# Four bias stores and eight bias reads issued by GpSimd in place of SyncE, in an attention and feed-forward kernel on one core

## The chip, the cores and the metric

One core of one Trainium2 chip runs the whole kernel. The metric is device time in microseconds (us), the median of a few executions; beside it stands one profiled execution, whose trace is what is read here. The engines are named as in the trace: PE (TensorE), ACT (ScalarE), DVE (VectorE), POOL (GpSimd) and SP (SyncE, which only issues transfers here).

## The reference

Attention with a bias that depends on the two positions, then a feed-forward layer over the 2304 tokens:

```python
B, H, S, D = 4, 8, 576, 64
scores = q @ k^T / sqrt(D)
x      = log1p(|i - j|) / log1p(max(i, 1))          # i query, j key
bias   = relu(x * w1 + b1) @ w2                     # hidden 32, one value per head
attn   = softmax(scores + bias)
x      = (attn @ v) as (B*S, H*D)                   # 2304 x 512
h      = x @ w_in;  out = (h * sigmoid(h)) @ w_out  # d_ff 2048
```

## The kernel before

All instructions are laid out by a planner (`Plan`, line 203) before the program is built: every step is an operation with a due time, its engines, and the buffers it reads and writes; `order` (line 286) simulates them with estimated durations and writes them out in the order that results. Each engine then works through its own list in that order, and waits at an instruction until what it needs is there. A table (`SHIFT`, line 40) moves the due times of single groups.

The bias is made on the chip once. It has 36 tiles of 16 query rows each, `bias_tile(st, t0)` (line 487). Four `bias_f` steps (line 503 on ACT or line 505 on DVE) compute the hidden layer from a table of logarithms, SBUF to SBUF; matmuls (line 511) bring in w2; two evictions (`bias_ev`, line 518 on ACT or line 520 on DVE) scale the result out of PSUM into a tile `bsb` of 128 partitions by 591 values; and a store (`bias_st`, line 522) writes that tile to a scratch tensor in DRAM, `bias_d[c]`, with c = st // 8. In DRAM the rows are skewed, so that a later read with a shifted row pitch gives the bias of each query row by key. Chunks c = 0 to 3 have 128 query rows (8 tiles each); chunk c = 4 has the last 64 rows (tiles 32 to 35). Chunk 4 is done first: `PHASES` (line 26) begins with it, then come 0, 1, 2, 3 for batches 0 and 1, and later the two other batches.

In a phase, `visit` goes over four pairs of heads (hp) and the batches. `bias_of(hp, c, t0)` (line 640) gives the bias tile of a head pair, read from DRAM. For c = 4 the two heads of a pair lie in the two halves of the partitions, so there are two reads per pair (`ld_bias2`, line 654, 64 partitions by 576 values each) and, ahead of them, two memsets on POOL (lines 650 and 651) that fill the margins of the tile. For c < 4 there is one read per pair (line 657). A read must wait for the stores of all tiles of its chunk: it depends on `bias_b[c]`.

In `chunk` (line 746) the step "max" (line 795, on DVE) adds the scores in PSUM to the bias tile and takes the row maximum; "exp" (line 802, ACT), transposes (line 811, PE), evictions (lines 446 and 448) and the product with v (line 683, PE) follow. The feed-forward part (lines 867, 890, 974, 1058) is PE work beside and behind the attention.

Before the change all transfers are issued by SP, in one list. Each of its transfers signals one of eight semaphores in turn (DMAHW0 to DMAHW7 in the rows of the program), and an issue that is to use one of them again waits until the transfer eight places earlier has landed.

Of the kernel before, what the change touches and what calls it, by code (L numbers as in the profile page):

```python
# [387 lines left out]
def attention_moe_kernel(ctx: ExitStack, tc: tile.TileContext, q, k, k0, v, small, w_in, w_out, lut, ident_d, out):  # L388
    nc = tc.nc
    V, A, G, T, SP = nc.vector, nc.scalar, nc.gpsimd, nc.tensor, nc.sync  # L390
# [14 lines left out]
    def bias_at(c, at, dims, h=0, n=H):  # L405
        t = bias_d[c].rearrange("h i p -> (h i p)")
        size = bias_d[c].shape[1] * (BW + 15)
        return bass.AP(tensor=t.tensor, offset=t.offset + h * size + at, ap=[x or [size, n] for x in dims])

    bias_b = [Buf(None) for _ in range(5)]  # L410
# [12 lines left out]
    def buf(tag, shape, dtype=F32):  # L423
        return Buf(tag, shape, dtype)

    def bank(tag, n):
        return Buf(tag, banks=n)

    def tl(b):
        if b.banks:  # L430
            return psum[:, b.at, :] if b.banks == 1 else psum[:, b.at:b.at + b.banks, :].rearrange("p a n -> p (a n)")
        if b.t is None:
            n = 1
            for x in b.shape[1:]:
                n *= x
            flat = pools[b.tag].tile([128, sizes[b.tag]], b.dtype, tag=b.tag, name=b.tag)
            b.t = flat[:, 0:n]
            if len(b.shape) == 3:
                b.t = b.t.rearrange("p (a n) -> p a n", a=b.shape[1])
            if len(b.shape) == 4:  # L440
                b.t = b.t.rearrange("p (a b n) -> p a b n", a=b.shape[1], b=b.shape[2])
        return b.t
# [10 lines left out]
    def op(kind, where, prio, reads=(), writes=(), shy=6.0):  # L453
        def add(fn):
            plan.op(kind, where, prio, fn, reads, writes, shy=shy)
            return fn
        return add

    def load(kind, prio, writes, fn, bytes, reads=(), plain=False):
        plan.op(kind, ("SP", 0.45 if plain else 0.55), prio, fn, reads, writes, bytes)  # L460
# [26 lines left out]
    def bias_tile(st, t0):  # L487


        plan.group()  # L490
        lo, hi = 16 * st + 15, S - 16 * st
        n = max(lo + 1, hi)
        bps = bank("B", 1 if n <= 512 else 2)
        Fs = [buf("G", [128, 2, n]) for _ in range(2)]
        bsb = buf("G", [128, BW])
        fat = lambda i: tl(Fs[i // 2])[:, i % 2, :]
        for ig in range(4):
            @op("bias_f", {"ACT": 0.2 + n * 0.00083, "DVE": 0.13 + n * 0.00053},
                t0 + 0.3 * ig, reads=[lut_b, (cb, 0)], writes=[(Fs[ig // 2], ig)])
            def _(e, g=4 * st + ig, ig=ig):  # L500
                src = tl(lut_b)[:, 0:n]
                if e == "ACT":
                    A.activation(out=fat(ig), in_=src, func=AF.Relu, bias=beta(g))
                else:
                    ENG[e].tensor_scalar(out=fat(ig), in0=src, scalar1=beta(g), scalar2=0.0, op0=ALU.add, op1=ALU.max)

        @op("bias_mm", ("PE", n * 0.00167 + 0.1), t0 + 1.8, reads=[(Fs[i // 2], i) for i in range(4)] + [(cb, 0)], writes=[bps])
        def _(e):
            for x in range(0, n, 512):
                for ig in range(4):  # L510
                    T.matmul(out=tl(bps)[32 * ig:32 * ig + 32, x:min(n, x + 512)], lhsT=w2bd(), rhs=fat(ig)[:, x:min(n, x + 512)],
                             start=True, stop=True)

        @op("bias_ev", {"ACT": 0.3 + BW * 0.00083, "DVE": 0.24 + BW * 0.00103}, t0 + 2.5, reads=[bps, cb], writes=[bsb])
        def _(e):
            for x, d, w in ((tl(bps)[:, lo:0:-1], 0, lo), (tl(bps)[:, 0:hi], lo, hi)):
                if e == "ACT":
                    A.activation(out=tl(bsb)[:, d:d + w], in_=x, func=AF.Copy, scale=scale(st))
                else:
                    V.tensor_scalar_mul(out=tl(bsb)[:, d:d + w], in0=x, scalar1=scale(st))  # L520

        load("bias_st", t0 + 3.2, [(bias_b[st // 8], st)], lambda e: SP.dma_start(
            out=bias_at(st // 8, 16 * (st % 8) * (BW + 15), [[BW + 16, 16], None, [1, BW]]), in_=tl(bsb)), 302592, reads=[bsb])


# [61 lines left out]
    def keys(b, hp, t0):  # L587
        plan.group()
        if b in RAW:
            kst = buf("G", [128, 704])  # L590
            load("ld_k", t0 - 14, [kst], lambda e: SP.dma_start(out=tl(kst), in_=k0[b, hp]), 360448)
            return kst, kst, kst
        src = k[b, hp].rearrange("d a n -> d (a n)")
        kst = buf("G", [128, 2 * S])
        load("ld_k", t0 - 14, [kst], lambda e: SP.dma_start(out=tl(kst), in_=src), 589824)

        khi, klo = buf("G", [128, 2 * S], F32R), buf("G", [128, 2 * S], F32R)

        @op("k_hi", {"ACT": 1.06, "DVE": 0.67}, t0 - 8, reads=[kst], writes=[khi])
        def _(e):  # L600
            copy(e, tl(khi), tl(kst))

        for a in range(2):
            @op("k_lo", {"POOL": 1.37, "DVE": 0.68}, t0 - 6 + 0.1 * a, reads=[kst, khi], writes=[(klo, a)])
            def _(e, a=a):
                sub(e, tl(klo)[:, S * a:S * a + S], tl(kst)[:, S * a:S * a + S], tl(khi)[:, S * a:S * a + S])
        return kst, khi, klo

    def values(b, hp, t0):
        plan.group()  # L610
        vs = buf("M", [128, 640])
        src = v[b, hp].rearrange("p s a d -> p (s a d)")
        load("ld_v", t0 - 6, [vs], lambda e: SP.dma_start(out=tl(vs), in_=src[:, 0:640]), 327680, plain=True)
        return vs
# [20 lines left out]
            sub(e, tl(qs)[HALF[1], :], tl(qst)[HALF[1], 0:n], tl(qs)[HALF[1], :])  # L635
        return qst, qs

    biases = {}

    def bias_of(hp, c, t0):  # L640

        if (hp, c) in biases:
            return biases[hp, c]
        last = c == 4
        bias = biases[hp, c] = buf("G", [128, S + 64 if last else 2 * S])
        dims = [[BW + 15, bias_d[c].shape[1]], [1, S]]
        if last:
            @op("bias_pad", ("POOL", 0.25), t0 - 9.1, writes=[bias])
            def _(e):
                G.memset(tl(bias)[HALF[0], S:], -1e30)  # L650
                G.memset(tl(bias)[HALF[1], 0:64], -1e30)

            for a, x in enumerate(HALF):
                load("ld_bias2", t0 - 9, [(bias, a)], lambda e, a=a, x=x: SP.dma_start(
                    out=tl(bias)[x, 64 * a:64 * a + S], in_=bias_at(4, 15, [None, *dims], 2 * hp + a, 1)), 147456, reads=[bias_b[4]])
        else:
            load("ld_bias", t0 - 9, [bias], lambda e: SP.dma_start(
                out=tl(bias), in_=bias_at(c, 15, [dims[0], None, dims[1]], 2 * hp, 2)), 589824, reads=[bias_b[c]])
        return bias
# [86 lines left out]
    def chunk(b, hp, c, i, x0, d0, kv, qs, pt, sm, sq, col, t0):  # L746
# [4 lines left out]
        heads = 1 if last else 2  # L751
        width = S + 64 if last else S
        bias, p = bias_of(hp, c, t0), buf("G", [128, heads * width])
        sps = [bank("S", 2) for _ in range(heads)]
        if last and b in QUAD:
# [423 lines left out]
    for c, some in PHASES:  # L1179
        if c not in made:  # L1180
            for i, st in enumerate(range(8 * c, min(8 * c + 8, 36))):
                bias_tile(st, (t - B1 if made else -60) + BD * i)
        made.add(c)
        for hp in range(4):
            for b in some:
                if (b, hp) not in kv:
                    kv[b, hp], vs[b, hp] = keys(b, hp, t), values(b, hp, t)
            t = visit(hp, [(b, (c,), kv[b, hp], vs[b, hp]) for b in some], first, sq, t)
        biases.clear()
        t += GAP0  # L1190
    factors(first, sq, t)

# [93 lines left out]
```

## Time and profile before

| | |
|---|---|
| median of 3 runs | 682.07 us (681.1 to 683.33) |
| the profiled execution | 683.77 us, of which the span of its trace is 681.8 us |
| PE busy | 669.7 us, 98% of the span |
| DVE / ACT busy | 567.8 us (83%) / 423.6 us (62%) |
| POOL busy | 120.6 us (18%) |
| DMA | 186.49 MB, mean 274 GB/s, all issued by SP |

Times in the trace are counted from the start of the span. A row of the timeline merges neighbouring instructions of one line: start, time until the last of them ends, engine, line, operation, output<-input, count, and in brackets the idle time of that engine ahead of it with what ended it. SP's rows are the issuing alone; a transfer goes on after its issue, and "to landing" is the time from issue until its semaphore says that all of it has arrived.

### The profile page before, as it was taken

Reading aid. Unit: us, or ns where it says so; the run is one execution under the profiler, and the core shown is the slowest. Engines: PE = TensorE matmul, PEld = TensorE weight load, DVE = VectorE, ACT = ScalarE, POOL = GpSimd, SP = SyncE. Lnnn points to the kernel's source line nnn. Section 1 sums busy time; section 2 is a strip of 40 time slices with the busy share of each in tenths; the row PEclk is TensorE's granted clock in tenths of the full one; section 3 lists DMA queues with packets and bytes.
Section 4 is the critical chain, followed back from the end, with each engine's and each line's share of the span. In section 5 each row is a group of like instructions: output and inputs, shape, how many; then the busy total and the mean of one; then the engine's idle time right before and its main releaser. Section 6 shows DMA issues by size and latency. Waiting matters only on the chain.

```text
span 681.8 us, 15118 instructions
## 1 busy us (share of the span) xinstructions
PE 669.7 (98%) x5500; PEld 568.5 (83%) x5500; DVE 567.8 (83%) x1240; ACT 423.6 (62%) x901; POOL 120.6 (18%) x119
## 2 busy tenths in 40 slices
PE   9899999999999999999999999999999999999997
PEld 5356767777878788787877899999999999999997
DVE  7899696788999998898977788988899566995775
ACT  8899685678898787697755346565574423632331
POOL 1000000204241222114303223230131000300120
PEclk9999999999999999999999999999999999999999
DMA  8989846788699874889547969899899888799921
GB/s 289 313 281 317 273 136 203 242 257 259 224 332 299 314 240 161 289 257 323 158 135 258 357 253 324 303 307 309 295 361 395 289 342 283 281 372 351 402 91 62
DMA packets 84073, 186.49 MB, mean 274 GB/s; under 512 B 11552, under 2 KB 34464, under 8 KB 84000
## 3 DMA queue, kind: packets, MB, share of 16 engines
q1 hardware_dynamic: 84000, 185.54, 79.3%
q8 instruction: 43, 0.70, 0.4%
q14 instruction: 30, 0.25, 0.1%
HBM read 139.93 MB, written 45.57 MB: 272 GB/s over the span
## 4 chain that ended last, share of the span: by engine, by line
PE 56%; DVE 2%; DMA 1%; ACT 1%; issue 0%; ACTq 0%; DVEq 0%
PE psum L1058 18%; PE psum L974 17%; PE psum L867 7%; PE psum L890 6%; PE psum L683 3%; PE psum L811 2%; PE psum L788 2%; DMA G<-win_d 1%; ACT G L802 0%; PE psum L762 0%; DVE G L451 0%; ACT G L446 0%; DVE G L1037 0%; ACT w L533 0%; DVE w L546 0%
## 5 line engine op out<-in xcount | busy, mean ns | idle before, releaser
L802 ACT ACTIVATE G<-G,sm 128x576 f32<-128x576 f32 (+1 forms) x144 | 111.5, 777 | 29.5 <-DVE sm L795 28.7
L1058 PE MATMUL psum<-G 128*128 128x256 f32 x864 | 119.2, 283 | 0.3 <-DVE G L451 0.3
L795 DVE CUSTOM_DVE_ANT_0 G<-psum,G 128x576 f32<-128x576 f32 (+1 forms) x144 | 105.4, 759 | 9.5 <-PE psum L788 4.0
L1058 PEld LDWEIGHTS psum<-G 128*128 128x128 f32 x864 | 110.5, 192 | 0.7 <-DVE G L451 0.5
L811 PEld LDWEIGHTS psum<-ident,G 128*128 128x128 f32 x656 | 73.0, 141 | 25.9 <-ACT G L802 8.6
L811 PE MATMUL psum<-ident,G 128*128 128x128 f32 x656 | 91.9, 277 | 1.6 <-ACT G L802 0.8
L683 PE MATMUL psum<-pt,M 128*64 128x128 f32 (+3 forms) x1120 | 85.8, 306 | 0.2 <-ACT pt L446 0.2
L974 PE MATMUL psum<-pt,G 128*128 128x256 f32 x576 | 81.1, 284 | 0.0
L683 PEld LDWEIGHTS psum<-pt,M 128*64 128x64 f32 x1120 | 62.0, 137 | 21.9 <-issue 3.9
L867 PE MATMUL psum<-M,G 128*128 128x384 f32 x384 | 76.4, 341 | 0.0
L890 PE MATMUL psum<-G,M 128*128 128x512 f32 x288 | 75.2, 398 | 0.0
L974 PEld LDWEIGHTS psum<-pt,G 128*128 128x128 f32 x576 | 74.3, 192 | 0.6 <-ACT M L446 0.2
L451 POOL TENSOR_TENSOR G<-w,G 128x512 fp32r<-128x512 f32 x27 | 36.1, 1345 | 184.7 <-ACT G L446 158.2
L446 ACT ACTIVATE pt<-psum 128x512 f32<-128x512 f32 (+3 forms) x100 | 51.7, 535 | 26.4 <-PE psum L811 20.1
L867 PEld LDWEIGHTS psum<-M,G 128*128 128x128 f32 x384 | 65.9, 188 | 2.3 <-issue 1.0
L448 DVE COPY pt<-psum 128x640 f32<-128x640 f32 (+3 forms) x92 | 53.9, 602 | 14.2 <-PE psum L811 8.5
L890 PEld LDWEIGHTS psum<-G,M 128*128 128x128 f32 x288 | 51.6, 188 | 9.9 <-issue 1.3
L446 ACT ACTIVATE G<-G 128x512 fp32r<-128x512 f32 (+1 forms) x56 | 38.0, 694 | 23.0 <-DVE G L1037 19.5
L1010 ACT ACTIVATE M<-M 128x512 f32<-128x512 f32 x24 | 15.2, 631 | 54.4 <-DVE M L1001 54.4
L446 ACT ACTIVATE G<-w 128x512 fp32r<-128x512 f32 x64 | 39.4, 625 | 11.3 <-DVE w L551 5.4
L788 PE MATMUL psum<-G,M 128*128 128x288 f32 x256 | 45.8, 309 | 0.4 <-DVE pt L448 0.2
L788 PEld LDWEIGHTS psum<-G,M 128*128 128x128 f32 x256 | 36.6, 188 | 7.4 <-DVE sm L795 2.2
(100 smaller groups left out, 1056.7 us busy)
## 6 DMA issues: line engine op xcount, KB each, us to landing
G<-ts_d SPq DMA_DIRECT2D x48, 512.0 KB, 5.6
G<-win_d SPq DMA_DIRECT2D x40, 512.0 KB, 6.7
G<-bias_d SPq DMA_DIRECT2D x32, 576.0 KB, 5.8
G<-us_d SPq DMA_DIRECT2D x32, 512.0 KB, 6.4
bias_d<-G SPq DMA_DIRECT2D x36, 295.5 KB, 5.2
G<-in_w_out_dram SPq DMA_DIRECT2D x16, 512.0 KB, 6.0
G<-in_w_in_dram SPq DMA_DIRECT2D x16, 512.0 KB, 5.1
win_d<-G SPq DMA_DIRECT2D x16, 512.0 KB, 5.5
```

Source lines behind the costliest of these rows:

```text
L446: A.activation(out=out, in_=in_, func=AF.Copy)
L448: ENG[e].tensor_copy(out=out, in_=in_)
L451: ENG[e].tensor_tensor(out=out, in0=in0, in1=f(in1), op=ALU.subtract)
L683: T.matmul(out=tl(o)[x, d:d + n], lhsT=tl(vs)[:, (s + 1) % 5 * 128 + 64 * a:(s + 1) % 5 * 128 + 64 * a + 64], rhs=tl(pt)[:, s + 5 * a if s ...
L788: T.matmul(out=s[:, hf, 0:288], lhsT=tl(qs)[:, x0 + 128 * a:x0 + 128 * a + 128], rhs=tl(part)[:, S * a + 288 * hf:S * a + 288 * hf + 288], ...
L795: V.tensor_tensor_reduce(out=mine(p, a).rearrange("p (a n) -> p a n", a=2), in0=tl(sps[a]).rearrange("p (a n) -> p a n", a=2)[:, :, 0:widt ...
L802: A.activation(out=mine(p, a), in_=mine(p, a), func=AF.Exp, scale=-1.0, bias=tl(sm)[:, i + a:i + a + 1], accum_out=tl(sq)[:, col + 4 * a:c ...
L811: T.transpose(out=tl(tp)[:, 128 * s:128 * s + 128], in_=tl(p)[:, 128 * (s0 + s):128 * (s0 + s) + 128], identity=ident)
L867: T.matmul(out=tl(hp)[:, 0:TB], lhsT=tl(wr)[:, x, 128 * cc:128 * cc + 128], rhs=tl(xs[cc])[:, y, :], start=(cc + m == 0), stop=(cc == NC - ...
L890: T.matmul(out=tl(acc[i]), lhsT=tl(gg)[:, x, 128 * i:128 * i + 128], rhs=tl(wo[fi])[:, y, :], start=(fi == 0 and m == 0), stop=(fi == NF - ...
L974: T.matmul(out=half(i), lhsT=tl(w)[:, x, off + 128 * cc:off + 128 * cc + 128], rhs=tl(b)[:, at, y, :], start=(fresh and cc + n == 0), stop ...
L1058: T.matmul(out=tl(c)[:, 256 * i:256 * i + 256], lhsT=tl(g)[:, a, x + 128 * i:x + 128 * i + 128], rhs=tl(w)[:, b, y:y + 256], start=(fresh ...
```

## The change

The four stores of tiles 32 to 35 and the eight reads of chunk 4 in the first phase are issued by GpSimd (`G`) instead of SyncE. For the reads, `queue` is `G` as long as no phase is finished (`started` is empty); the second round of reads of chunk 4, for the other two batches, stays on SP. The planner still counts the twelve as SP's work, so it writes the program in the same order as before; each instruction only goes to the other engine's list.

```diff
@@ bias_tile
-        load("bias_st", t0 + 3.2, [(bias_b[st // 8], st)], lambda e: SP.dma_start(
+        load("bias_st", t0 + 3.2, [(bias_b[st // 8], st)], lambda e: (G if st >= 32 else SP).dma_start(
             out=bias_at(st // 8, 16 * (st % 8) * (BW + 15), [[BW + 16, 16], None, [1, BW]]), in_=tl(bsb)), 302592, reads=[bsb])
@@
-    biases = {}
+    biases, started = {}, []
@@ bias_of
         last = c == 4
+        queue = SP if started else G
@@
-                load("ld_bias2", t0 - 9, [(bias, a)], lambda e, a=a, x=x: SP.dma_start(
+                load("ld_bias2", t0 - 9, [(bias, a)], lambda e, a=a, x=x: queue.dma_start(
                     out=tl(bias)[x, 64 * a:64 * a + S], in_=bias_at(4, 15, [None, *dims], 2 * hp + a, 1)), 147456, reads=[bias_b[4]])
@@ the loop over PHASES
         biases.clear()
+        started.append(c)
```

Two lines are added above line 795 by the end of the file, so that line 654 becomes 655, and 795 becomes 796.

Where the instructions stand, on POOL. The names: bias_d4 is chunk 4's scratch tensor, G_240, G_257, G_272 and G_301 are the four finished tiles, G_163, G_394, G_475 and G_541 the bias tiles of the four head pairs, sq two small accumulators. Before, POOL's list from the accumulators on is:

```order
L711 MEMSET sq_168 128x128
L650 MEMSET G_394 64x64 [waits DVE_49,PE_49,Activation_49]
L651 MEMSET G_394 64x64 [waits Pool_49]
L650 MEMSET G_475 64x64 [waits DMAHW3_49,DVE_49]
L651 MEMSET G_475 64x64
L650 MEMSET G_541 64x64 [waits DMAHW4_49,DVE_49]
L651 MEMSET G_541 64x64
```

and with the change:

```order
L522 DMA bias_d4_103<-G_240 16x8x591 [waits DVE_49]
L522 DMA bias_d4_103<-G_301 16x8x591 [waits DVE_49]
L655 DMA G_163<-bias_d4_103 64x576 [waits DMASW2_49,DMASW3_49,DMASW1_49,DMASW0_49]
L651 MEMSET G_394 64x64 [waits PE_49,Activation_49]
L652 MEMSET G_394 64x64 [waits Pool_49]
L655 DMA G_163<-bias_d4_103 64x576
L655 DMA G_394<-bias_d4_103 64x576
L651 MEMSET G_475 64x64 [waits DMAHW7_49,DVE_49]
L652 MEMSET G_475 64x64
L655 DMA G_394<-bias_d4_103 64x576
L651 MEMSET G_541 64x64 [waits DMAHW6_49,DVE_49]
```

The first read now waits for the four stores (semaphores DMASW0 to DMASW3) in POOL's own list, and two memsets stand between the two reads of the first tile.

On SP, the stretch from the first of these stores to the first of these reads, before:

```order
L522 DMA bias_d4_103<-G_240 16x8x591 [waits DMAHW5_49,DVE_49]
L623 DMA M_267<-in_q_dram 128x192 [waits DMAHW6_49]
L522 DMA bias_d4_103<-G_257 16x8x591 [waits DMAHW7_49,DVE_49]
L522 DMA bias_d4_103<-G_272 16x8x591 [waits DMAHW0_49,DVE_49]
L613 DMA M_298<-in_v_dram 128x640 [waits DMAHW1_49]
L522 DMA bias_d4_103<-G_301 16x8x591 [waits DMAHW2_49,DVE_49]
L522 DMA bias_d0_99<-G_325 16x8x591 [waits DMAHW3_49,DVE_49]
L623 DMA M_351<-in_q_dram 128x192 [waits DMAHW4_49]
L591 DMA G_366<-in_k0_dram 128x704 [waits DMAHW5_49]
L623 DMA M_372<-in_q_dram 128x192 [waits DMAHW6_49]
L591 DMA G_386<-in_k0_dram 128x704 [waits DMAHW7_49,PE_49]
L654 DMA G_163<-bias_d4_103 64x576 [waits DMAHW2_49,DMAHW0_49]
```

and with the change:

```order
L623 DMA M_267<-in_q_dram 128x192 [waits DMAHW5_49]
L613 DMA M_298<-in_v_dram 128x640 [waits DMAHW6_49]
L522 DMA bias_d0_99<-G_325 16x8x591 [waits DMAHW7_49,DVE_49]
L623 DMA M_351<-in_q_dram 128x192 [waits DMAHW0_49]
L591 DMA G_366<-in_k0_dram 128x704 [waits DMAHW1_49]
L623 DMA M_372<-in_q_dram 128x192 [waits DMAHW2_49]
L591 DMA G_386<-in_k0_dram 128x704 [waits DMAHW3_49,PE_49]
```

The loads between the stores move up, and no longer stand behind a wait for DVE until the store of tile 0 (bias_d0).

On DVE, the stretch up to the first "max", before:

```order
L520 TENSOR_SCALAR G_429<-psum_98,cb_170 128x79 [waits DMAHW5_49,PE_49]
L520 TENSOR_SCALAR G_429<-psum_98,cb_170 128x512
L505 TENSOR_SCALAR G_442<-lut_sb_161,cb_170 128x432 [waits Activation_49]
L505 TENSOR_SCALAR G_442<-lut_sb_161,cb_170 128x432
L505 TENSOR_SCALAR G_445<-lut_sb_161,cb_170 128x480 [waits DVE_49,Activation_49]
L505 TENSOR_SCALAR G_455<-lut_sb_161,cb_170 128x480 [waits DMAHW2_49]
L505 TENSOR_SCALAR G_455<-lut_sb_161,cb_170 128x480
L795 ISA G_466,sm_467<-psum_98,G_163 128x640 [waits DMAHW0_49,DVE_49,DMAHW1_49,Activation_49,Pool_49]
```

and with the change:

```order
L520 TENSOR_SCALAR G_429<-psum_98,cb_170 128x79 [waits PE_49,Activation_49]
L520 TENSOR_SCALAR G_429<-psum_98,cb_170 128x512
L505 TENSOR_SCALAR G_442<-lut_sb_161,cb_170 128x432 [waits DMASW2_49]
L505 TENSOR_SCALAR G_442<-lut_sb_161,cb_170 128x432
L505 TENSOR_SCALAR G_445<-lut_sb_161,cb_170 128x480 [waits Activation_49]
L505 TENSOR_SCALAR G_455<-lut_sb_161,cb_170 128x480 [waits DMASW3_49,DVE_49]
L505 TENSOR_SCALAR G_455<-lut_sb_161,cb_170 128x480
L796 ISA G_466,sm_467<-psum_98,G_163 128x640 [waits DMASW4_49,DVE_49,DMASW5_49,Activation_49,Pool_49]
```

DVE's order is the same; two of its `bias_f` steps now wait for a store issued by POOL (they reuse its buffer), and the "max" waits for the two reads issued by POOL.

## Rows read from the trace of the kernel before

**Rows 1.** The page's head, and busy time in four stretches (us).

```profile
span 681.8 us, 15118 instructions
...
20.00:30.00 10.00, 8.21 (x74) 2.87 (x66) 8.19 (x23) 7.91 (x20) 0.29 (x2) 1.00 1.04 323
50.00:60.00 10.00, 9.10 (x110) 4.75 (x108) 8.86 (x24) 9.53 (x25) 0.00 (x0) 1.00 1.02 337
70.00:80.00 10.00, 9.87 (x102) 6.46 (x99) 6.07 (x14) 6.87 (x16) 0.00 (x0) 1.00 0.71 239
60.00:110.00 50.00, 49.87 (x523) 36.20 (x516) 38.64 (x94) 37.99 (x88) 0.00 (x0) 1.00 0.73 234
```

**Rows 2.** Waits of DVE for transfers, 0 to 70 us: total, times, longest.

```profile
DVE G L795 <- DMA G<-bias_d: 1.7, 1, 1.7
DVE G L520 <- DMA bias_d<-G: 0.9, 1, 0.9
```

**Rows 3.** Timeline of DVE, 7 to 25 us, and 51 us.

```profile
7.22 1.82 DVE L520 TENSOR_SCALAR G<-psum,cb 128x527 f32<-128x527 f32 x4
8.96 0.51 DVE L505 TENSOR_SCALAR G<-lut_sb,cb 128x576 f32<-128x576 f32 x1
9.38 0.95 DVE L520 TENSOR_SCALAR G<-psum,cb 128x559 f32<-128x559 f32 x2
10.25 0.94 DVE L505 TENSOR_SCALAR G<-lut_sb,cb 128x576 f32<-128x576 f32 x2
11.11 0.95 DVE L520 TENSOR_SCALAR G<-psum,cb 128x575 f32<-128x575 f32 x2
11.97 0.91 DVE L505 TENSOR_SCALAR G<-lut_sb,cb 128x560 f32<-128x560 f32 x2
...
17.58 1.98 DVE L505 TENSOR_SCALAR G<-lut_sb,cb 128x512 f32<-128x512 f32 x5
19.48 0.95 DVE L520 TENSOR_SCALAR G<-psum,cb 128x79 f32<-128x79 f32 x2
20.35 1.93 DVE L505 TENSOR_SCALAR G<-lut_sb,cb 128x432 f32<-128x432 f32 x5
24.01 0.82 DVE L795 CUSTOM_DVE_ANT_0 G<-psum,G 128x640 f32<-128x640 f32 x1 [1.74 <-DMA G<-bias_d]
...
51.02 0.96 DVE L520 TENSOR_SCALAR G<-psum,cb 128x335 f32<-128x335 f32 x2 [0.93 <-DMA bias_d<-G]
```

**Rows 4.** Timeline of SP's issues.

```profile
8.20 0.65 SPq L522 DMA_DIRECT2D bias_d<-G  x1
...
9.57 1.31 SPq L522 DMA_DIRECT2D bias_d<-G  x2
...
12.08 2.22 SPq L522 DMA_DIRECT2D bias_d<-G  x2
...
17.80 1.14 SPq L654 DMA_DIRECT2D G<-bias_d  x2
```

**Rows 5.** Instructions on bias_d, 0 to 90 us: issue time (ns, min/median/max), landing.

```profile
L522 SPq DMA_DIRECT2D bias_d<-G x32: 518/549/1393, 8.2 to 81.0; - x32
...
L654 SPq DMA_DIRECT2D G<-bias_d x8: 472/589/1275, 17.8 to 35.3; - x8
...
DMA to landing us min/median/max: 3.9/5.4/7.9
```

**Rows 6.** Landing of line 522's transfers, 0 to 20 us.

```profile
DMA to landing us min/median/max: 5.6/5.6/5.6
```

**Rows 7.** Timeline of POOL.

```profile
8.88 0.14 POOL L650 MEMSET G<- 64x64 f32 x1 [7.15 <-PE psum L511]
9.08 0.47 POOL L651 MEMSET G<- 64x64 f32 x1
18.49 1.16 POOL L650 MEMSET G<- 64x64 f32 x1 [8.94 <-DMA bias_d<-G]
19.68 0.15 POOL L651 MEMSET G<- 64x64 f32 x1
```

**Rows 8.** The page's groups: POOL's costliest line (busy us, mean ns).

```profile
L451 POOL TENSOR_TENSOR G<-w,G 128x512 fp32r<-128x512 f32 x27 | 36.1, 1345 | 184.7 <-ACT G L446 158.2
```

## The prediction

> **What bounds the kernel now.** I read the stretches first. From 60 us on PE is the bound: it is busy 49.87 of the 50 us from 60 to 110, while DVE and ACT have room (38.64 and 37.99) [rows 1]; the page's 98% for the whole span says the same. So nothing that only speeds up a transfer after 60 us is worth anything. The twelve moved transfers lie before 40 us, where the picture differs: PE is busy 8.21 of 10 us from 20 to 30, DVE 8.19 and ACT 7.91, and from 50 to 60 it is 9.10, 8.86 and 9.53 [rows 1]. DVE and ACT make the bias there and PE waits for them. Since PE has no room afterwards, I count a shift of DVE before 60 us as a shift of the end, one for one.
>
> Second, the waits: in the first 70 us DVE waits for transfers only twice, 1.7 us at its first "max" (line 795) for the read of the bias, and 0.9 us at 51 us for a store that frees a buffer [rows 2]. Their sum, 2.7 us, is all that faster transfers can give here.
>
> Third, the chain behind the first wait. Tile 35, the last of chunk 4, is evicted by the two L520 that start at 11.11 and end at 12.06; SP issues its store at 12.08 [rows 3, 4]. That store took 5.6 us to land [rows 6], until about 17.7, and SP issues the two reads from 17.80 on, the second at about 18.4; the "max" starts at 24.01, when DVE had been idle for 1.74 us [rows 3, 4]. So SP issues these stores within 0.2 us of the data (the first at 8.20, DVE's first pair being half of a row of 1.82 us from 7.22): there is almost no queueing ahead of the issue to win. What is long is the landing, two times 5.6 us or so, with the DMA engines full (share 1.04 from 20 to 30 us [rows 1]).
>
> **The change, part by part.** *Removed from SP:* 12 issues, at medians of 549 ns (4 stores) and 589 ns (8 reads) [rows 5], 6.9 us of SP's time. SP computes nothing, so this is worth only what waits for SP later: the 0.93 us at 51.02, which may go wholly, or stay since that store has its own landing time. I take half, -0.4 us, ends 0 and -0.9.
>
> *Added to POOL:* 12 issues. The trace of before has no transfer issued by POOL. Bounds for the time one takes there: 0.14 us, POOL's undisturbed small memset [rows 7], and 1.35 us, its pass over 128 partitions by 512 values [rows 8]. I take SP's 0.55 for the same transfer as the nearest row. POOL has little else then: four pairs of memsets, so its work as such is hidden.
>
> *Landing.* Issued on another queue, the same bytes go through the same busy DMA engines. Bounds are the quickest and slowest of the bias transfers, 3.9 and 7.9 us [rows 5]. I take 4.75, the middle between 3.9 and the 5.6 that SP's stores took [rows 6], since a transfer of POOL's need not stand behind eight of SP's.
>
> *POOL beside DVE.* This is the term that speaks against the change. The same memset of 64 by 64 took 0.14 us at 8.88, beside DVE's L520 (from PSUM), and 1.16 us at 18.49, beside five L505 (SBUF to SBUF) from 17.58 to 19.56; it ended at 19.65, when they had. The one at 9.08 took 0.47 and ended with the L505 of 8.96 to 9.47 [rows 3, 7]. So POOL's writes give way to a running series of L505, and POOL gets on in the L520 between. No row shows whether the issue of a transfer does the same; I take it that it does, at the start of each. The Trainium skill (SBUF — State Buffer, section "SBUF: two separate sides") says that it does: descriptors of a DMA issued from GpSimd are written by GpSimd's cores, and VectorE's two-port modes lock them out, for which it advises SP or ACT as issuer. Its example is 620 ns alone against about 3100 beside VectorE; by that, two such issues on the chain would add some 5 us as an estimate.
>
> *The sum on the chain.* Tile 35 is ready at 12.06, but L505 runs from 11.97 to 12.88, so its store starts at 12.88 and lands at 12.88 + 4.75 = 17.63, about as before. The five L505 from 17.58 to 19.56 have then just begun: the first read starts at 19.56 and is issued by 20.1; two memsets of 0.15 us stand before the second read, which comes up at 20.45. The next five L505 begin at 20.35. Either the second read slips in, and lands at 20.45 + 4.75 = 25.2, or it waits until 22.28 and lands at 27.0. The "max" started at 24.01, so this is +1.2 or +3.0 us. With a landing of 3.9 both are 0.85 less; and if nothing gives way, -1.74 at the most, where DVE itself becomes free (22.28). I take +1.2: the two instants lie 0.1 us apart, and POOL, once in, follows on without a gap (19.65 to 19.68 [rows 7]).
>
> *The other reads.* The six reads for the other head pairs are needed from 32 us on, when POOL has had 8 us for them; no row shows DVE waiting for one, and I cost them at nothing. If their cover goes, each can hold up an L505 by its issue, 6 x 0.55 = 3.3 us at most.
>
> *New waits on DVE:* two L505 of the series at 20.35 wait for the third and fourth store. Landed at 17.63, these cost nothing; behind them the whole of DVE's list would stand, including the "max" itself.
>
> Sum: +1.2 - 0.4 = **+0.8 us**. The profiled execution took 683.77, of which the span is 681.8 [rows 1] and 1.97 lies around it; with the change 684.6. It stands 1.7 us above the median of 682.07, so for the median I forecast **682.9**; with the ends of the terms where it holds, 680.4 to 684.1.
>
> **Rivals.** *The own queue wins (faster).* POOL's issue is not held up by L505 and its transfers don't stand behind SP's. Then the store lands at 12.06 + 4.75 = 16.8, the reads are issued at once and land by 16.8 + 0.55 + 0.3 + 4.75 = 22.4, and the "max" follows DVE directly: -1.6 to -1.74, and up to -0.93 for the wait at 51 us: 682.07 - 2.7 = 679.4. For it: the chain is two landings long, and every store of SP's there took 5.6 us against a minimum of 3.9. Against it: the memset rows [rows 7], and the full DMA engines. Arbitration by turns between queues would favour it; that is what the Trainium skill states (DMA: Bandwidth & Descriptors, section "Queues, rings and completion order"), and no row here shows it.
>
> *The lock-out is dear (slower).* The place is the second read, the price the wait until 22.28, and it decides as soon as POOL comes up for that read while the series of 20.35 is running, or a store is issued in two pieces: the gaps between L505 from 8.96 to 13 are 0.8 us long, so an issue of over 0.8 us doesn't fit into one. Then the "max" starts at 27.0 or later, +3.0 (685.1), and with an issue of 1.35 us and the six further reads in DVE's way up to +3.8 + 3.3 = +7 (689). For it: the 1.16 us memset. Against it: a series of L505 ends by itself once DVE reaches the "max", and POOL then has it free.
>
> *It does nothing.* Same engines, same bytes, and issues that were hidden on either queue: 682.07. The Trainium skill has this as a rule too (DMA: Bandwidth & Descriptors, section "Issuing engines are not separate DMA queues"): issuing from several engines saves the sequencer's time only. Against it: landing and the memsets both depend on the queue.
>
> **How the numbers follow.** A difference of 0.3%, 2.05 us, is about what a measurement of this kernel can tell from none. The forecast has 0.37 (all within). The own queue has 0.27; it needs nearly both waits to pass 2.05 us, since 1.74 alone doesn't, so I put 0.20 of it at faster and 0.07 within. The lock-out has 0.31, all slower. Doing nothing has 0.05, within. So faster 0.20, same 0.49, slower 0.31. The range must reach into both neighbours: 679.6, just short of both waits gone, to 687.5, most of the way through the lock-out's 685.1 to 689.
>
> **What would show it.** Right: POOL's memsets and issues bunch up behind L505 series; the first read is issued near 19.6 and the "max" starts at 24.5 to 25.5, with DVE's wait of 1.74 grown to about 3; SP's loads of k, q, v between 14 and 20 us are earlier. Wrong on the fast side: a "max" at 22.3 with no wait ahead of it and landings of POOL's transfers clearly under 5.6 us. Wrong on the slow side: a "max" after 26.5, L505 stretched while POOL issues, or a wait of an L505 for a POOL store. The argument as a whole is wrong if the "max" moves and the end doesn't move with it.

## The result, and the profile after

| | before | with the change |
|---|---|---|
| median, same chip | 681.59 us (680.97 to 683.33) | 687.43 us (686.92 to 688.55, 4 runs) |
| the profiled execution | 683.77 us, span 681.8 | 688.55 us, span 686.8 |

The ratio is 1.0084, with a 95% interval of 1.0059 to 1.0108: slower by 5.8 us. A later repetition on another chip (a3 below) gave 1.0068 [1.0047, 1.0089], or 4.4 us. The forecast was 682.9; what happened has the sign and the size of the rival "the lock-out is dear" (685.1 to 689), but not quite its mechanism. The median lies 0.07 us inside the upper end of the range, 687.5, and that end was drawn through this rival's prices and not through the terms of the forecast: that the range held is luck.

The head and the stretches, to be held against [rows 1] (columns: length, PE, PE's weight loads, DVE, ACT, POOL, granted clock, DMA share, GB/s):

```profile
span 686.8 us, 15132 instructions
...
20.00:30.00 10.00, 5.12 (x48) 1.68 (x52) 4.26 (x12) 4.76 (x12) 6.27 (x14) 0.89 0.95 314
30.00:40.00 10.00, 9.46 (x102) 4.31 (x94) 8.28 (x24) 8.21 (x21) 0.00 (x0) 0.77 1.02 332
50.00:60.00 10.00, 9.15 (x145) 5.13 (x142) 9.12 (x30) 9.64 (x25) 0.00 (x0) 1.00 1.00 324
60.00:110.00 50.00, 49.87 (x494) 34.80 (x490) 40.89 (x101) 41.28 (x95) 0.00 (x0) 1.00 0.72 228
```

From 50 us on PE does what it did: 9.15 us against 9.10 from 50 to 60, and 49.87 of 50 from 60 to 110, as before. From 20 to 30 us PE's work falls from 8.21 to 5.12 and DVE's from 8.19 to 4.26, and from 30 to 40 us PE runs at a mean of 0.77 of its full 2.4 GHz, that is, partly at 1.2 GHz. Most of the loss lies before 40 us.

DVE's waits from 0 to 70 us, as in [rows 2]:

```profile
DVE G L796 <- DMA G<-bias_d: 5.7, 1, 5.7
```

The wait for the bias has grown from 1.7 to 5.7 us; no row for a wait of line 520 for a transfer is left. DVE's timeline, against [rows 3]:

```profile
17.59 1.98 DVE L505 TENSOR_SCALAR G<-lut_sb,cb 128x512 f32<-128x512 f32 x5
...
20.35 1.93 DVE L505 TENSOR_SCALAR G<-lut_sb,cb 128x432 f32<-128x432 f32 x5
28.01 0.82 DVE L796 CUSTOM_DVE_ANT_0 G<-psum,G 128x640 f32<-128x640 f32 x1 [5.74 <-DMA G<-bias_d]
```

The series of L505 start and last as before (17.58, 20.35; 1.98, 1.93 us): DVE is not slowed by POOL, it is only kept waiting at the first "max", 28.01 instead of 24.01. POOL's timeline:

```profile
8.48 1.65 POOL L522 DMA_DIRECT2D bias_d<-G  x2 [6.74 <-DVE G L520]
10.63 0.68 POOL L522 DMA_DIRECT2D bias_d<-G  x1 [0.50 <-DVE G L520]
12.36 0.66 POOL L522 DMA_DIRECT2D bias_d<-G  x1 [1.04 <-DVE G L520]
20.49 1.89 POOL L655 DMA_DIRECT2D G<-bias_d  x1 [7.48 <-DMA bias_d<-G]
22.37 0.17 POOL L651 MEMSET G<- 64x64 f32 x1
...
22.69 1.03 POOL L655 DMA_DIRECT2D G<-bias_d  x2
```

POOL's queue sees the semaphores of the stores at 19.4 to 19.9 us, by the view of line 655 alone. The landing of the stores, in that of line 522 from 0 to 20 us:

```profile
DMA to landing us min/median/max: 7.6/8.4/9.1
```

Three things are to be read here. The stores land in 7.6 to 9.1 us, against 5.6 in [rows 6]. The first read is started 0.6 us after the last semaphore (19.9), takes 1.89 us where a free issue takes 0.52 (half of the 1.03 at 22.69), and ends at 22.38, when the series of L505 does (20.35 + 1.93). And the second read lands only some 5 us after its issue.

The landing of the stores is less of the change's doing than these rows suggest. In a second profile of the kernel before (b2, more on it below), with everything on SP, the landing of line 522's transfers from 0 to 20 us and SP's row for the two reads are:

```profile
DMA to landing us min/median/max: 7.0/7.3/7.6
...
19.08 1.13 SPq L654 DMA_DIRECT2D G<-bias_d  x2
```

Of the five profiles with these stores on SP two have 5.6 us (the first, and e2_reads) and three have 6.7 to 7.6 (b2, e9_ctl, e10_behind). The profile that the forecast read was a quick one in this place. The packets of the change from 8 to 12 us fit a store that waits behind SP's earlier loads (q1 carries SP's transfers, q0 POOL's: packets, MB, share of the 16 DMA engines): POOL begins its first store at 8.48, and the view has no row for q0.

```profile
q1 hardware_dynamic: 624, 1.24, 96.2%
```

SP's issues, against [rows 4], where the two reads stand at 17.80:

```profile
13.79 0.64 SPq L522 DMA_DIRECT2D bias_d<-G  x1
...
16.86 0.44 SPq L613 DMA_DIRECT2D M<-in_v_dram  x1
17.35 0.42 SPq L591 DMA_DIRECT2D G<-in_k_dram  x1
18.56 0.56 SPq L522 DMA_DIRECT2D bias_d<-G  x1
```

A load of v, a load of k and a store of chunk 0 (320, 352 and 295 KB) are out on SP's queue before POOL has issued its first read. In the kernel before they stand behind the reads in the list. This turned out to be the largest single part.

How the shift carries to the end: the start of the same instruction in each profile, less its start in a second profile of the kernel before (b2: 682.26 us, span 680.3, nearer to the median than the 683.77 read for the forecast).

| at (us in b2) | 24.18, first "max" | 32.73, third | 52.77, ninth | 140.9 | 349.0 | 647.2 |
|---|---|---|---|---|---|---|
| the first profile of before | -0.17 | -0.17 | +0.84 | +0.68 | +0.72 | +1.52 |
| the change | +3.83 | +4.75 | +4.74 | +4.87 | +4.83 | +6.14 |
| the change again (a3) | +2.46 | +3.36 | +3.35 | +3.18 | +3.09 | +3.81 |
| e10_behind (below) | +1.89 | +2.67 | +2.66 | +2.51 | +2.43 | +2.47 |

What DVE loses at its first "max", and in these profiles another 0.8 to 0.9 us by the third, stays to the end. The last 0.7 to 1.3 us come after 350 us and vary between executions of one kernel (0.72 to 1.52 in that of before); I don't assign them.

### The profile page after: what moved, and what is told of

Same layout as the page of the kernel before. It is cut to its first block, busy times and chain, and to the rows that moved or that the text cites. A ratio compares the mean times of both kernels' runs of the same rounds, so it can differ in the third digit from the quotient of the medians.

```text
span 686.8 us, 15132 instructions
## 1 busy us (share of the span) xinstructions
PE 670.4 (98%) x5500; PEld 569.2 (83%) x5500; DVE 567.1 (83%) x1240; ACT 423.6 (62%) x901; POOL 127.9 (19%) x131
## 4 chain that ended last, share of the span: by engine, by line
PE 56%; DVE 1%; DMA 1%; ACT 1%; issue 0%; SPq 0%; ACTq 0%; DVEq 0%
PE psum L1059 18%; PE psum L975 17%; PE psum L868 7%; PE psum L891 6%; PE psum L684 3%; PE psum L812 2%; PE psum L789 2%; DMA ts_d<-G 1%; ACT G L803 0%; PE psum L763 0%; DVE G L1038 0%; ACT w L533 0%; ACT G L446 0%; DVE w L546 0%; DVE G L921 0%
## 5 line engine op out<-in xcount | busy, mean ns | idle before, releaser
L446 ACT ACTIVATE G<-G 128x512 fp32r<-128x512 f32 (+1 forms) x56 | 38.0, 694 | 23.6 <-DVE G L1038 19.5
```

Of the source, the lines that this page charges most:

```text
L446: A.activation(out=out, in_=in_, func=AF.Copy)
```

## The experiments

**Which half.** e1_stores moves only the four stores, e2_reads only the eight reads.

```diff
@@ e1_stores
-        queue = SP if started else G
+        queue = SP
@@ e2_reads
-        load("bias_st", t0 + 3.2, [(bias_b[st // 8], st)], lambda e: (G if st >= 32 else SP).dma_start(
+        load("bias_st", t0 + 3.2, [(bias_b[st // 8], st)], lambda e: SP.dma_start(
```

> Only the four stores go to GpSimd, the eight reads stay on SyncE. If the later landing of the stores is one part of the loss and the locked-out read another: the fourth store lands near 19.9 us as with the full change, SyncE issues both reads at once, and the first max starts near 26.0 (24.0 before, 28.0 with the full change); the time lies about half way, 684 to 685 us. If the lock-out at the reads is the whole loss: max near 24.3 and the time of before. If the stores are the whole loss: max near 28 and the full +5.8 us.

> Only the eight reads go to GpSimd, the four stores stay on SyncE. The fourth store lands near 17.7 us as before. Lock-out theory: the first read comes up just inside the L505 series of 17.6 to 19.6 us, its issue ends at about 19.6, and the second read is issued near 20.4 or, if it misses the gap, near 22.3; max at 25.4 to 27.6. Rival (no lock-out, the reads' issue costs 0.5 us each): max at 24.0 plus or minus 0.5 and the time of before within 1 us.

Measured: e1_stores 682.96 us, ratio 1.0021 [1.0006, 1.0036]; e2_reads 686.88 us, ratio 1.0071 [1.0044, 1.0097]. So the reads carry the loss; with the stores alone little is lost. My split for e1_stores was wrong (a "max" near 26.0, 684 to 685 us; it came at 22.96). The profile of e2_reads is of the fastest of its five runs (684.57 us); it has its "max" at 25.23 and no issue of a read over 0.73 us, so it does not explain that median. The timeline of e1_stores shows the reads issued by SP, and the "max":

```profile
19.06 1.14 SPq L655 DMA_DIRECT2D G<-bias_d  x2
20.30 0.53 SPq L613 DMA_DIRECT2D M<-in_v_dram  x1
...
22.96 0.82 DVE L796 CUSTOM_DVE_ANT_0 G<-psum,G 128x640 f32<-128x640 f32 x1 [0.47 <-DMA G<-bias_d]
```

SP's queue sees the semaphores at 18.9 to 19.0 us there. The landing of line 655's transfers in e1_stores, 18 to 22 us:

```profile
DMA to landing us min/median/max: 3.1/3.1/3.2
```

And DVE's waits for stores in e1_stores, 30 to 60 us:

```profile
DVE G L505 <- DMA bias_d<-G: 0.9, 2, 0.7
DVE G L520 <- DMA bias_d<-G: 0.7, 1, 0.7
```

SP starts its read within 0.15 us of the semaphore, both reads go back to back ahead of the load of v, and they land in 3.1 to 3.2 us, the shortest of all. The "max" comes 1 us earlier than before, and yet the time is not better: by 43 us nothing of it is left in the profile, and between 30 and 60 us stand 1.6 us of waits for stores that free a buffer.

**The lock-out.** e4_slow gives DVE's `bias_f` of tiles 6 and 9 (the series at 20.4) a second tensor operand, zero, so that they compute the same in another form; e9_ctl does that to the kernel before. a3, and earlier a2, are the change once more, and b2 the kernel before once more.

```diff
-    ENG[e].tensor_scalar(out=fat(ig), in0=src, scalar1=beta(g), scalar2=0.0, op0=ALU.add, op1=ALU.max)
+    if st in (6, 9):
+        V.scalar_tensor_tensor(out=fat(ig), in0=src, scalar=beta(g), in1=zero.bitcast(F32)[:, 0:1].to_broadcast([128, n]), op0=ALU.add, op1=ALU.max)
+    else:
+        V.tensor_scalar(out=fat(ig), in0=src, scalar1=beta(g), scalar2=0.0, op0=ALU.add, op1=ALU.max)
```

> The full change, but the five L505 of the series at 20.35 us (and the others of those two tiles) are written as a scalar_tensor_tensor with a zero operand, which computes the same and runs slower (about 0.6 us each instead of 0.38). Lock-out theory: the first read's issue takes 0.5 to 0.7 us instead of 1.89, and the max starts near 26.7 instead of 28.0 although DVE works longer. Rival (the first read is slow for a reason of its own, such as being the first of its kind on this queue): it keeps 1.9 us and the max stays at 28 or later.

> Control: the kernel before, with DVE's bias_f steps of tiles 6 and 9 in the form with a second tensor operand and all transfers on SyncE. Theory (that form helped the change only by letting GpSimd through): here it gives nothing, 681.5 to 683.5, the first 'max' within 0.7 us of 24.0; the memset that took 1.16 us beside the series at 17.6 takes 0.2. Rival (the form itself makes the kernel faster, or shifts DVE's order): 2 us faster than before, about 679.7.

> The change as it is, again, beside the other two on one chip. Theory: 686.9 to 688.6, the first 'max' at 27.5 to 28.1 with GpSimd's read or memset held to the end of a series of L505 near 20.4. Rival (the slow dispatch was an accident of two executions): a 'max' before 27 and a time of 685 to 686.

Measured: e4_slow 685.46 us, 1.0051 [1.0033, 1.0069]; e9_ctl 682.11, 0.9997 [0.9985, 1.0010]; a3 686.15, 1.0068 [1.0047, 1.0089]; single runs: a2 687.39, b2 682.26. Three timelines follow, of a2, a3 and e4_slow, each with rows of POOL and then of DVE.

```profile
19.67 0.55 POOL L655 DMA_DIRECT2D G<-bias_d  x1 [6.61 <-PE psum L511]
...
20.43 1.98 POOL L652 MEMSET G<- 64x64 f32 x1
...
20.39 1.93 DVE L505 TENSOR_SCALAR G<-lut_sb,cb 128x432 f32<-128x432 f32 x5
27.79 0.82 DVE L796 CUSTOM_DVE_ANT_0 G<-psum,G 128x640 f32<-128x640 f32 x1 [5.47 <-DMA G<-bias_d]
```

```profile
20.10 0.55 POOL L655 DMA_DIRECT2D G<-bias_d  x1 [6.68 <-PE psum L511]
...
20.95 1.20 POOL L655 DMA_DIRECT2D G<-bias_d  x2
...
20.88 1.93 DVE L505 TENSOR_SCALAR G<-lut_sb,cb 128x432 f32<-128x432 f32 x5
26.64 0.82 DVE L796 CUSTOM_DVE_ANT_0 G<-psum,G 128x640 f32<-128x640 f32 x1 [3.84 <-POOL G L652]
```

```profile
20.59 1.03 POOL L658 DMA_DIRECT2D G<-bias_d  x2
...
20.40 3.13 DVE L506 SCALAR_TENSOR_TENSOR G<-lut_sb,cb,zero 128x432 f32<-128x432 f32 x5
26.66 0.82 DVE L799 CUSTOM_DVE_ANT_0 G<-psum,G 128x640 f32<-128x640 f32 x1 [3.13 <-DMA G<-bias_d]
```

In a2 a memset of 0.15 us comes up just after the series has begun and takes 1.98 us, to its end; in the first profile it was the read. In a3 POOL was already going when the series began, and its two issues took 1.20 us together beside it, against 1.03. Then the "max" stands at 26.64, as in e4_slow (26.66), where issues beside DVE take 0.52. (The row of a3 names a memset as what ended DVE's wait; those of its own tile were long done, and what it waited for is the read.) So the lock-out is real and worth 1.2 to 1.4 us at the "max" where it strikes (28.01 and 27.79 against 26.6), and it doesn't strike each time: my expectation of a3 fell in that. In e9_ctl the same form, with all on SP, gives nothing by itself; the memset that I meant to see there came up only after its series and tells nothing. The Trainium skill (SBUF — State Buffer, section "SBUF: two separate sides") has the other engine blocked for as long as a two-port operation of VectorE runs; beside an operation with two inputs from SBUF only those steps of GpSimd are held up that read SBUF. The rows of a2 and of e4_slow agree, while the 1.20 us for two issues in a3 do not fit full blocking. In e5_hold2 below the third read came up right behind the second and was held all the same (1.89 us), so what decides is not settled. Even without the lock-out most of the loss remains: 1.0051. The intervals of e4_slow and a3 overlap, and their "max" stands at the same place; what differs between their profiles behind it is PE's clock, which stayed at 1.00 from 20 to 40 us in e4_slow.

**SP held where it was held before.** First theory for the slow landings: SP, no longer waiting for the tiles, fills the DMA engines early. e3_hold lets SP store a piece of 16 by 128 of each of the four tiles at the old place of the store; e5_hold2 also reads 16 by 16 values of bias_d at the old place of each read; e8_both is e5_hold2 with e4_slow's form. The pieces are extra work; the rest is computed in full.

```diff
@@ e3_hold, e5_hold2, e8_both
-        load("bias_st", t0 + 3.2, [(bias_b[st // 8], st)], lambda e: (G if st >= 32 else SP).dma_start(
...
+        def store(e):
+            if st >= 32:
+                SP.dma_start(out=hold_d[st - 32], in_=tl(bsb)[0:16, 0:128])
+            (G if st >= 32 else SP).dma_start(
...
@@ e5_hold2, e8_both
+                def read(e, a=a, x=x):
+                    if queue is G:
+                        SP.dma_start(out=hold_s[2 * hp + a], in_=bias_at(4, 15, [None, [4 * (BW + 15), 16], [1, 16]], 2 * hp + a, 1))
+                    queue.dma_start(out=tl(bias)[x, 64 * a:64 * a + S], in_=bias_at(4, 15, [None, *dims], 2 * hp + a, 1))
...
```

> The full change, but SyncE still waits for each of the four tiles, since it stores 16 by 128 values of it (8 KB) to a tensor that nobody reads, in the place where the whole store stood. Theory that the stores land late because SyncE's loads, no longer held back, run ahead of them in the DMA engines: landing falls from 7.6-9.1 us to about 5.6, the fourth store lands near 18 us, and the max starts at 25.4 to 27.6 (the reads still meet L505). Rival that GpSimd's queue itself is served slowly: landing stays over 7.5 us and the max stays near 28.

> The full change, but SyncE keeps a tiny transfer in the place of each of the twelve: 8 KB of each tile to a tensor that nobody reads, and 16 by 16 values ahead of each of GpSimd's eight reads, which wait for the four stores as the reads on SyncE did. So SyncE's list and its waits are as before; only the payloads go through GpSimd's queue. Theory that the loss comes from SyncE running ahead while GpSimd waits: the two reads land 3.3 to 4.5 us after their issue (5.3 with the full change), the max starts at 24 to 25 and the time is within 1.5 us of before. Rival that GpSimd's queue is slow in itself: the reads take over 5 us, the max starts after 25.5 and the time stays 3 us or more above before.

> Both supposed costs taken out at once: SyncE issues a tiny transfer behind the same wait wherever one of the twelve went to GpSimd, so that its later loads do not run ahead, and DVE's bias_f steps of tiles 6 and 9 use a form with a second tensor operand, beside which GpSimd's steps ran at 0.5 us each. All twelve transfers are still on GpSimd. Theory (late dispatch by the lock-out plus slow landings beside SyncE's early loads make nearly all of it): first read issued at 19.4 to 19.8, second by 21.0, landing of the pair 4 to 4.5 us, the first 'max' at 25.0 to 25.8, the time 683.0 to 684.5. Rival (GpSimd's queue is itself slow to start and land a transfer, whatever else runs): the 'max' stays at 26.3 or later and the time at 685 or more.

Measured: e3_hold 686.00 us, 1.0067 [1.0046, 1.0088]; e5_hold2 686.66, 1.0073 [1.0052, 1.0094]; e8_both 686.32, 1.0064 [1.0049, 1.0079]. In e3_hold and e5_hold2 POOL's stores land sooner (medians 6.5 and 5.8 us, against 8.4), but the time does not improve: the "max" stands at 26.39 and 26.63. e5_hold2, from which I expected a "max" at 24 to 25, and e8_both, from which I expected 683.0 to 684.5, show their rivals' numbers. The packets of e8_both show why. First the timeline of e8_both, POOL's rows and then SP's:

```profile
19.45 0.61 POOL L668 DMA_DIRECT2D G<-bias_d  x1 [6.17 <-DMA bias_d<-G]
...
20.37 1.03 POOL L668 DMA_DIRECT2D G<-bias_d  x2
...
19.93 0.37 SPq L623 DMA_DIRECT2D M<-in_v_dram  x1
20.34 0.43 SPq L601 DMA_DIRECT2D G<-in_k_dram  x1
```

Then the packets by queue in e8_both from 20.75 to 22 us and from 22 to 23.25 us:

```profile
q0 software_dynamic: 47, 0.15, 55.4%
q1 hardware_dynamic: 55, 0.12, 43.7%
...
q1 hardware_dynamic: 169, 0.41, 96.0%
q0 software_dynamic: 1, 0.00, 0.0%
```

POOL's first read, issued before v and k, has moved its 0.15 MB by 22 us, sharing the engines with q1; the shortest landing of e8_both's first four reads is 3.3 us, like SP's in e1_stores: POOL's queue is not slow by itself. The second, issued at 20.37, after the load of v at 19.93 and 0.03 us after that of k, waits while q1 moves 0.41 MB in 1.25 us with one packet of q0, and the "max" waits for it until 27.48, some 7 us after its issue (the median of the four is 6.8). My holds kept SP back at the reads but let v and k slip in between the first and the second read.

The same order can be seen the other way round, in the change from 14 to 15.5 us: SP's store of 13.79 is out, POOL's stores of 8.48 to 12.36 are not yet through, and POOL's have the engines.

```profile
q0 software_dynamic: 144, 0.54, 93.5%
q1 hardware_dynamic: 21, 0.04, 6.9%
```

And in e4_slow, where no series locks POOL out, from 20.5 to 22.5 us q1 alone is served, though POOL's first read was issued at 19.74:

```profile
q1 hardware_dynamic: 296, 0.70, 97.7%
```

**PE's clock.** e7_warm runs 30 matmuls of zeros on PE during the wait, ahead of the third group of scores.

```diff
...
+            if quads == 3:
+                ...
+                for _ in range(30):
+                    T.matmul(out=psum[:, tp.at, 0:256], lhsT=zero[:, 0:128], rhs=zero[:, 0:256], start=True, stop=True)
```

> The full change, and 30 small matmuls on zeros for TensorE in the wait between the last bias matmul near 23.5 us and the first max. Theory that about 0.9 us of the loss is TensorE's granted clock, which fell to 0.77 from 30 to 40 us after the idle stretch: the clock stays at 1.00, the shift against before stays at that of the max (4.0 and not 4.9 us) and the time falls by about 1 us, to 686.5. Rival: the clock is no part of it and the time stays at 687.4.

Measured: 685.42 us, 1.0059 [1.0038, 1.0079]. The two stretches 20 to 30 and 30 to 40 us:

```profile
20.00:30.00 10.00, 9.74 (x97) 4.90 (x89) 5.86 (x16) 6.23 (x15) 4.99 (x14) 1.00 1.03 364
30.00:40.00 10.00, 8.85 (x106) 3.94 (x103) 9.05 (x29) 8.87 (x23) 0.00 (x0) 1.00 0.95 305
```

The clock stays at 1.00, and the shift against b2 does not grow from the first "max" (+2.24) to the third (+2.30), where it grew by 0.92 in the change, 0.62 in a2, 0.90 in a3 and 0.78 in e10_behind. In e4_slow the clock stayed at 1.00 too, and the shift did not grow (+2.48 at both). So the idle PE costs 0.6 to 0.9 us on top of the wait, by the profiles. POOL was not locked out in this profile either ("max" at 26.42). Against a3 the median is 0.7 us better, within both spreads, and the interval overlaps those of a3 and of the first measurement: in the time this gain is not shown.

**Order of issue alone.** e10_behind is the kernel before, all on SP, with the first two reads behind the three transfers that got ahead of them in the change.

```diff
...
+        if plan.kinds[i] == "ld_bias2" and n < 2:
+            n += 1
+            first.append(plan.ops[i][2])
+            continue
+        plan.ops[i][2](e)
+        if first and "SP" in plan.ops[i][0]:
+            n += 1
+            if n == 5:
+                for step in first:
+                    step(None)
+                first = []
```

> The kernel before, all transfers on SyncE, but the first two reads of the bias stand behind the three transfers that followed them in SyncE's list (a load of v, a load of k, a store of tile 1 of chunk 0: 320, 352 and 295 KB). The packets of the runs so far show GpSimd's transfers starting only when SyncE's earlier issued ones have drained, and in the change these three are issued before the reads. Theory (transfers are served about in the order of their issue, on whatever queue, and the change lost part of its time because these three got ahead of the reads): the reads are issued at 19.1 to 20.0, at most 0.8 us later than where SyncE issues them in the kernel before, but land 5 to 6.5 us after it instead of 3.3 to 5; the first 'max' at 25.8 to 27.0, the time 683.5 to 685.5, though nothing is on GpSimd. Rival (it is GpSimd's queue that starts and lands slowly, and the three don't matter): the 'max' follows the issue as before, 24.0 to 25.0, the time 681.5 to 683.

Measured: 684.57 us (683.69 to 685.93), 1.0033 [1.0021, 1.0046] against 682.23. The timeline of e10_behind, SP's rows and the "max":

```profile
18.04 0.33 SPq L613 DMA_DIRECT2D M<-in_v_dram  x1
18.52 0.33 SPq L591 DMA_DIRECT2D G<-in_k_dram  x1
18.94 0.53 SPq L522 DMA_DIRECT2D bias_d<-G  x1
19.72 1.14 SPq L654 DMA_DIRECT2D G<-bias_d  x2
...
26.07 0.82 DVE L795 CUSTOM_DVE_ANT_0 G<-psum,G 128x640 f32<-128x640 f32 x1 [2.81 <-DMA G<-bias_d]
```

With no transfer on POOL the "max" comes at 26.07 and the end 2.3 us later, as the theory had it. The landing of the two reads themselves is not in this trace. The second is issued at about 20.3 and the "max" waits for it, so it took at most 5.8 us; with these reads ahead of v, k and the store SP's took 5.5 to 5.7 in the first profile of before, 4.4 to 4.5 in b2 and 3.1 to 3.2 in e1_stores. Against b2 the reads are issued 0.64 us later (19.72 against 19.08), and the rest of the 1.9 us by which the "max" moved is landing. The 967 KB ahead of the reads are 0.99 MB; at the 314 GB/s of the change's stretch from 20 to 30 us that is 3.2 us of the DMA engines' time as an estimate, more than the "max" lost, but of that order.

## Why the prediction was right or wrong

*What bounds the kernel now: right.* Before 60 us a shift of DVE is a shift of the end; the table shows it carried one for one. It is not so for a gain: the 1 us that e1_stores won at the "max" was gone by 43 us. There was no more than the two waits to win, and the chain of store and read is where it was decided.

*Removed from SP: this step failed.* The text took the 12 issues away as time that only SP loses: "SP computes nothing, so this is worth only what waits for SP later". What went was not time but a place in a queue. The reads had stood ahead of v, k and a store; without their waits SP put these three out at 16.86 to 18.56, before POOL's reads. The text even named the earlier loads as something to see, and gave them no price. Measured alone (e10_behind) it is 0.33% [0.21, 0.46], 2.3 us, half of what a3 lost and two fifths of the first measurement; 0.8 us of it comes behind the "max", with PE's clock.

*Landing: mis-sized.* I took 4.75 us for both landings, "since a transfer of POOL's need not stand behind eight of SP's". It does stand behind what SP issued earlier: the stores took 7.6 to 9.1, and the reads 5 us and more. But SP's own stores took up to 7.6 in b2, and the 5.6 of [rows 6] is the landing of two of the four stores alone, tile 35's not among them: it was no safe base, and much of this is no effect of the change: the last store was in at 19.9, 19.1 and 19.5 in the three profiles of the change, and at 19.0 in b2. Tile 35's store was begun at 12.36 and over at 13.02, where I had it start at 12.88, and POOL saw the last semaphore at 19.9, 7.5 us after 12.36. My bounds of 3.9 to 7.9 us for a landing were too narrow above. (The text's ends of 680.4 to 684.1 us are given without their sum; nothing here hangs on them.)

*POOL beside DVE: the mechanism right, and the instant as close as I had said.* The issue of a transfer is held by a series of L505 as the memset was. I placed the first read at 19.56, where the series of 17.58 ends, with the second at risk; in the first profile it was the first read that met the next series (20.49 against 20.35), in a2 the memset ahead of the second, in a3 neither. The price, 1.2 to 1.4 us, is near the 1.8 between my two cases.

*Price of an issue on POOL:* 0.52 to 0.68 us in the rows above, where I took 0.55: right, but for the 1.89 and one of the first two stores, 1.12 of their 1.65. Not counted was that POOL starts its read 0.6 us after the semaphore, where SP needs under 0.15.

*PE's clock: missing.* A longer wait at the "max" idles PE, and its clock fell to 0.77 from 30 to 40 us: 0.6 to 0.9 us in the three profiles of the change.

*The wait at 51 us, -0.4:* it went, as half expected, but b2, the kernel before once more, does not have it either, and the table's first line shows it as +1.0 between the third and the ninth "max" of the first profile alone. Nothing of it is owed to the change.

*The six other reads at nothing, and no wait of an L505 for a store:* right; no row of DVE's waits names either.

*The rivals.* "The lock-out is dear" has the outcome: its mark, a "max" after 26.5, was met in every profile of the change (28.01, 27.79, 26.64). But its mechanism is the smaller part, and without it the change still loses (1.0051 in e4_slow). "The own queue wins" fell on the DMA engines, not on POOL: by the Trainium skill (DMA: Bandwidth & Descriptors, section "Queues, rings and completion order") each DMA engine takes turns between the queues that have work; the windows of e4_slow and e8_both, 296 and 169 packets of one queue against 0 and 1 of the other with both issued, don't show such turns, while the window of e8_both before that, 47 against 55, is what turns would give.

Put together, for the first "max" of the change: order of issue +1.9 (e10_behind against b2), a remainder of about 0.6 (a3's +2.46 less that), the lock-out 1.4 (3.83 less 2.46), then 0.9 for the clock: 4.8 us at the third "max", where +4.75 was measured. I put the remainder down to POOL's later start, but the last store was also in later (19.5 in a3, 19.0 in b2), so that is argued and not shown. The parts come from single profiles and the sum uses the total for two of them, so it is a consistent account rather than four independent prices; tested by a kernel of its own are the order of issue, in the time, and the clock, in the profile alone. Restoring the order with the reads left on POOL (both issued back to back ahead of v and k) was not tried, so it is open whether the change could be made harmless. No version here beats the kernel before: the nearest are e9_ctl (0.9997) and e1_stores (1.0021).

## What to carry to other kernels

Where the DMA engines are full, an issue on a queue is also a place in line: before a transfer is moved to another engine's queue, list what on the old queue will now be issued ahead of it, and price those bytes at the DMA rate of that stretch. A wait that looks like a nuisance on SP may be what holds less urgent loads back, so a transfer on the critical chain should keep its place ahead of them, whichever engine issues it. Issues on POOL beside long SBUF-to-SBUF series of DVE are a gamble on instants 0.1 us apart.

## What the runs showed of the hardware that was not expected

- Of two queues, the transfers issued earlier were in three windows served nearly to the exclusion of the other, in both directions: 93.5% against 6.9% for POOL's earlier stores, 97.7% against nothing (e4_slow) and 96.0% against 0.0% (e8_both) for SP's earlier loads. In a fourth (e8_both, 20.75 to 22 us) the two shared, 55.4% to 43.7%. How the engines come to that order is not shown by these traces.
- A transfer issued by POOL can land as fast as SP's: 3.3 us (e8_both) against SP's 3.1 (e1_stores). Neither is a constant: POOL's reads have a median of 6.8 in e8_both, and the same two reads on SP took 4.4 to 4.5 in b2 and 5.5 to 5.7 in the first profile of before.
- POOL starts a read about 0.6 us after the last semaphore that it waited for (19.9 to 20.49 in the change), SP within 0.15 us (e1_stores). For POOL's store of tile 35 it was 0.3 us after DVE's eviction had ended (12.06 to 12.36).
- DVE's series keep their time beside POOL (1.93 us for the five L505 near 20.4 in the change, a2 and a3, as before); only POOL pays, and only at times: 1.89 and 1.98 us for a step of 0.5 or 0.15 when it comes up inside a series, 1.20 instead of 1.03 for two when POOL was under way before (a3).
